# Two one-column fills on GpSimd behind most indirect DMAs, with another table of order

## The chip, the cores and the metric

The kernel runs on one core of a Trainium2 chip. The metric is the time of one execution on the device, in microseconds (us). TensorE does the products, VectorE, ScalarE and GpSimd the work between them, and SyncE (SP) issues the plain loads and stores. GpSimd issues the indirect DMAs, those whose rows go to addresses that a table of indices gives.

## The reference

Two layers follow each other. The first is a gated linear recurrence over time, for each of 4 sequences of 5,056 steps and 256 channels; the second is a mixture of eight experts, over all 20,224 rows of the first one's result. A row whose score with `w_skip` is not above 0 is passed on as it is.

```python
log_a = c * sig_r * np.log(np.clip(a_base, 1e-06, 1.0 - 1e-06))[None, None, :]
a_t = np.exp(log_a)
norm = np.sqrt(np.maximum(1.0 - a_t * a_t, 1e-06))
x_gated = norm * sig_i * x
for t in range(S):
    h = a_t[:, t] * h + x_gated[:, t]
    y[:, t] = h
...
do_compute = x @ w_skip > 0
e_idx = np.argmax(logits, axis=1)          # logits = xc @ w_gate
for e in range(E):                         # E = 8, w1 256x1024, w2 1024x256
    mask = e_idx == e
    h = np.maximum(xc[mask] @ w1[e], 0.0)
    y[mask] = gate_w[mask, None] * (h @ w2[e])
out[do_compute] = xc + y
```

## The kernel before

**Groups and spans.** The rows are cut into groups of 512, and two groups make a span; there are 20 spans of eight tiles of 128 rows (the last has six), 158 tiles in all. For each group SP loads r, i and x (`load`), ScalarE applies tanh, exp and square root, TensorE turns the tiles so that time runs along the free axis (`across`), VectorE scans (`scan`), TensorE turns the result back (`back`), and ScalarE or VectorE copies it from PSUM into a row buffer `yr` (`copy`). GpSimd writes the row ids into that buffer (`ids`, an IOTA), SP stores the rows to `out` (`keep`). TensorE then computes the scores of the span, and VectorE and TensorE work out for each row its expert and its place in a sorted list.

**Sends.** When the places of a span are known, GpSimd sends its tiles, one indirect DMA each (`send`, L609), from `yr` into `xs`, a buffer in DRAM that is sorted by expert. There are three buffers `yr`, and a buffer is free again when its sends have read it.

**Slots.** A slot is one expert's work on 128 or 256 sorted rows: SP fetches them from `xs` (`fetch`, L692) into one of three buffers `xr`, TensorE turns them (`turn`, L706), ScalarE and VectorE make two half-precision parts (`turn_hi`, `turn_lo`), TensorE makes the first product (`mm1`, L727), ScalarE and VectorE the rectified parts (`relu`, L737, and `rest`, L741), TensorE the second product (`mm2`, L753), VectorE weighs it and adds the row (`weighed`, L763), and GpSimd puts 128 rows at a time at their place in `out` with an indirect DMA (`put`, L769). There are 48 slots in a fixed list, `STREAM`, which says for each the span that must have been sent, the expert and the number of rows; eight more follow, one for each expert, and a loop behind them for rows that are left. A buffer `xr` is free when its puts have been read out. 82 puts and 158 sends appear in the profile.

**Weights.** All of the experts' weights are loaded in pieces and turned into two half-precision parts in SBUF: the upper one by ScalarE (L670) or GpSimd (L672), the lower one by VectorE (L676).

**What sets the order.** Each step is a task of a plan, with the engine it runs on, the tasks that must come first and the buffers that it takes. Where a task may run on one of two engines, a letter of the string `ENGINES` says which. The table `ORDER` lists the numbers of all 2,780 tasks, and `Plan.order` goes through it and issues one after the other; each engine then does its instructions in that order:

```python
tasks = [self.tasks[int(i)] for i in ORDER.split()]
...
with tc.manual_schedule():
    for t in plan.order():
        t.f()
```

An instruction that waits holds up all that stands behind it in its engine's queue. Semaphores between engines are set by the framework from what each instruction reads and writes. Between the sends and the fetches they are declared by hand: a fetch waits for the last send of the span that it needs.

Of the kernel before, what the change touches and what calls it, by code (L numbers as in the profile page):

```python
# [22 lines left out]
    "PADDAAAAPAAAADAADAAADAAAAADAPAAAAADAAAAAAAAAAAAADAAAAAADAADADADAADDAADAAADDDAAADDAADAPAAADAAAAAAADPA"  # L23
    "AAADDAPDAADDAAAADAAAADDADAAAAADAAPADADAAPAAAAAAPPAAAPAAAAAAPAPAAAPPPAAAAAAAAPPPPPPAPPPPPPAAAAAAAPPAP"
# [190 lines left out]
def kernel(  # L215
# [12 lines left out]
    nc = tc.nc  # L228
# [372 lines left out]
    def count(s):  # L601
        nt = tiles_in(s)
        nc.vector.tensor_tensor(bases[s + 1], bases[s], vs.pop(s)["rk"][:, nt, :], op=ALU.add)
        known[s] = len(scattered), len(kept)

    def send(s, c):

        g, j = tile_at(s, c)
# [525 lines left out]
```

## Time and profile before

| | |
|---|---|
| time, median of 3 runs | 765.91 us (763.94 to 770.52) |
| time of the profiled execution | 764.61 us |
| span of its profile | 762.8 us |
| mean granted clock of TensorE | 0.948 |

The span runs from the first to the last instruction; the time of the profiled execution has 1.8 us around it. Engines are named PE (TensorE's products), PEld (its weight loads), DVE (VectorE), ACT (ScalarE), POOL (GpSimd) and SP. A row of a timeline ends with the idle time of the engine just before the instruction and with what released it; "issue" stands for time in which it waited for nothing that the profile shows. The granted clock is the share of TensorE's full speed that it was given, 1.00 for 2.4 GHz and 0.50 for 1.2.

### The profile page before, as it was taken

What the parts mean: (1) busy time and instruction counts of PE and PEld (TensorE: products, weight loads), DVE (VectorE), ACT (ScalarE), POOL (GpSimd) and SP (SyncE); (2) the same over time, 40 slices, a digit from 0 to 9 for tenths busy, and PEclk for the clock granted to TensorE, in tenths of its full rate; (3) what the DMA queues carried; (4) which work ended last, traced back from release to release, by engine and by line L of the source; (5) the groups of instructions that cost most, each with busy time, mean ns of one, the idle gap of its engine ahead of it and who ended that gap; (6) DMA issues with size and microseconds to landing.
All of it is one profiled execution on the core that took longest, in us unless ns stands there. A gap on an engine that the chain in (4) does not pass through costs nothing. (4 is left out here: it accounts for less than half of the span.)

```text
span 762.8 us, 16493 instructions
## 1 busy us (share of the span) xinstructions
PE 660.5 (87%) x6304; PEld 561.1 (74%) x6304; DVE 492.5 (65%) x1082; ACT 434.1 (57%) x622; POOL 307.1 (40%) x332
## 2 busy tenths in 40 slices
PE   2565887988989989898998997979987799999996
PEld 2343676877878977777777785769876698989996
DVE  2998885977887757785667576447664365454432
ACT  7889775877887557575664773453725123222231
POOL 5365634445355154375164434412553411321211
PEclk9878598999999999999899998989998899999999
DMA  8899967778876465385546471615353211232110
GB/s 322 311 286 330 301 211 242 236 233 271 273 263 229 158 223 179 111 300 189 196 125 181 165 265 59 198 34 185 133 162 96 83 57 37 97 138 71 56 40 20
DMA packets 72752, 134.73 MB, mean 177 GB/s; under 512 B 9912, under 2 KB 43176, under 8 KB 72672
## 3 DMA queue, kind: packets, MB, share of 16 engines
q1 hardware_dynamic: 60816, 112.84, 45.0%
q0 software_dynamic: 11584, 20.82, 7.7%
q8 instruction: 50, 0.82, 0.5%
q14 instruction: 30, 0.25, 0.1%
q10 hardware_dynamic: 272, 0.00, 0.0%
HBM read 89.75 MB, written 54.71 MB: 189 GB/s over the span
## 5 line engine op out<-in xcount | busy, mean ns | idle before, releaser
L727 PE MATMUL phs<-xhs,wsb 128*128 128x128 f16 (+1 forms) x2688 | 248.3, 248 | 19.6 <-issue 15.6
L753 PE MATMUL pos<-wsb,hps 128*128 128x256 f16 x1968 | 243.8, 276 | 13.7 <-ACT hps L737 5.4
L727 PEld LDWEIGHTS <-wsb 128*128 128x128 f16 x2688 | 210.8, 100 | 43.6 <-issue 28.9
L753 PEld LDWEIGHTS <-hps 128*128 128x128 f16 x1968 | 193.0, 99 | 46.6 <-issue 12.2
L609 POOL DMA_INDIRECT xs<-yr,di x158 | 176.4, 1117 | 110.2 <-issue 45.5
L737 ACT ACTIVATE hps<-phs 128x512 f16<-128x512 f32 x164 | 96.4, 595 | 192.0 <-PE phs L727 106.4
L769 POOL DMA_INDIRECT out_dram<-ots,xrs x82 | 87.0, 1061 | 267.7 <-DVE ots L763 163.8
L741 DVE SCALAR_TENSOR_TENSOR hps<-phs,hps 128x512 f16<-128x512 f32 x164 | 111.3, 685 | 82.1 <-ACT hps L737 77.3
L438 DVE TENSOR_TENSOR_SCAN a<-a,a,m 128x512 f32<-128x512 f32 (+1 forms) x78 | 99.7, 1288 | 0.4
L401 ACT ACTIVATE a<-pt,cc 128x512 f32<-128x512 f32 (+1 forms) x80 | 59.7, 773 | 34.5 <-PE pt L397 15.5
L397 PE MATMUL pt<-ident,i 128*128 128x128 f32 x316 | 53.6, 302 | 22.8 <-DVE i L427 9.8
L716 DVE SCALAR_TENSOR_TENSOR xhs<-pxs,xhs 128x256 f16<-128x256 f32 (+1 forms) x56 | 30.5, 546 | 53.9 <-ACT xhs L713 38.2
L763 DVE SCALAR_TENSOR_TENSOR ots<-pos,xrs 128x256 f32<-128x256 f32 x82 | 38.1, 478 | 40.6 <-PE pos L753 29.3
L397 PE MATMUL pt<-ident,r 128*128 128x128 f32 x316 | 52.2, 304 | 12.6 <-ACT r L388 11.6
L432 DVE SCALAR_TENSOR_TENSOR m<-m,pt 128x512 f32<-128x512 f32 x80 | 53.1, 672 | 14.2 <-PE pt L397 11.5
L397 PEld LDWEIGHTS pt<-ident,i 128*128 128x128 f32 x316 | 40.2, 155 | 29.5 <-issue 10.9
L455 PE MATMUL py<-ident,a 128*128 128x128 f32 x316 | 54.8, 302 | 4.7 <-DVE m L432 2.3
L713 ACT ACTIVATE xhs<-pxs 128x256 f16<-128x256 f32 (+1 forms) x56 | 27.0, 482 | 54.4 <-PE pxs L706 45.2
L427 DVE SCALAR_TENSOR_TENSOR i<-i,x 128x1024 f32<-128x1024 f32 (+1 forms) x40 | 49.6, 1242 | 8.0 <-ACT i L388 7.4
L397 PEld LDWEIGHTS pt<-ident,r 128*128 128x128 f32 x316 | 41.7, 159 | 15.4 <-issue 7.5
L455 PEld LDWEIGHTS py<-ident,a 128*128 128x128 f32 x316 | 45.6, 209 | 8.6 <-DVE m L432 3.0
L676 DVE SCALAR_TENSOR_TENSOR wsb<-w,wsb 128x512 f16<-128x512 f32 x64 | 44.0, 698 | 12.0 <-POOL wsb L672 6.2
(100 smaller groups left out, 577.9 us busy)
## 6 DMA issues: line engine op xcount, KB each, us to landing
r<-in_r_gate_dram SPq DMA_DIRECT2D x39, 512.0 KB
i<-in_i_gate_dram SPq DMA_DIRECT2D x39, 512.0 KB
x<-in_x_dram SPq DMA_DIRECT2D x39, 512.0 KB
out_dram<-yr SPq DMA_DIRECT2D x39, 512.0 KB
w<-in_moe_w_dram SPq DMA_DIRECT2D x64, 256.0 KB
xrs<-xs SPq DMA_DIRECT2D x26, 258.0 KB
xrs<-xs SPq DMA_DIRECT2D x30, 129.0 KB
xs<-yr,di POOLq DMA_INDIRECT x158
```

Of the source, the lines that this page charges most:

```text
L397: nc.tensor.transpose(tile_of(to[g, k], g, j), t[g][:, j, k * P:(k + 1) * P], ident)
L401: nc.scalar.activation(ta[g][:, k, :tiles_of(g) * P], tp.pop((g, k)), AF.Exp, scale=c, bias=c)
L427: nc.vector.scalar_tensor_tensor(ti[g], ti[g], 1.0, tx.pop(g), op0=ALU.add, op1=ALU.mult)
L432: nc.vector.scalar_tensor_tensor(m, m, 0.5e-3, tp.pop((g, k)), op0=ALU.max, op1=ALU.mult)
L438: nc.vector.tensor_tensor_scan(a, a, tm[g][:, k, :n], prev, op0=ALU.mult, op1=ALU.add)
L455: nc.tensor.transpose(pt[:, j, k * P:(k + 1) * P], tile_of(ta[g][:, k, :tiles_of(g) * P], g, 2 * h + j), ident,)
L609: i = nc.gpsimd.indirect_dma_start(out=xs[:, :], out_offset=bass.IndirectOffsetOnAxis(ap=vs[s]["di"][:, c:c + 1], axis=0), in_=yrow[g][:, ...
L727: nc.tensor.matmul(ph[:, c, :], lhsT=self.w.w1(k, part, q * self.fp + c), rhs=self.xx[:, xx, k, :], start=(n == 0), stop=(n == 3 * KD - 1),)
L737: nc.scalar.activation(hh[:, 0], self.h[q][0], AF.Relu)
L741: nc.vector.scalar_tensor_tensor(hh[:, 1], ph, 0.0, hh[:, 0], op0=ALU.max, op1=ALU.subtract)
L753: nc.tensor.matmul(self.po[:self.np, j, :], lhsT=hh[:, h, c, j * P:j * P + self.np], rhs=self.w.w2(f, part), start=(f == 0 and j == 0 and ...
L769: i = nc.gpsimd.indirect_dma_start(out=out[:, :], out_offset=bass.IndirectOffsetOnAxis(ap=self.at[:, j, :], axis=0), in_=self.ot.pop(j)[:s ...
```

## The change

A function `pause` makes two fills of the same one-column buffer `still` on GpSimd. It is called behind each send of span 4 and later and behind each put of slot 3 and later in the list (`PACE`). The loop's slots are not paced. The fills are not tasks of the plan; they are issued inside `send` and `put`. The strings `ENGINES` and `ORDER` are others, of which the diff shows the first line each; the tasks, the buffers and `STREAM` are the same.

```diff
--- before.py
+++ after.py
-    "PADDAAAAPAAAADAADAAADAAAAADAPAAAAADAAAAAAAAAAAAADAAAAAADAADADADAADDAADAAADDDAAADDAADAPAAADAAAAAAADPA"
...
+    "PAAAAADAPDAAADAAAAAADAAAADDAPAAAAAAAAAADDAAAADAADAAAADADAAADAADAADDDDAPAAADDAAAADADDPADADDDAADAAADAA"
...
 ORDER = """
...
+0 6 9 10 12 1620 17 7 1614 1605 1566 18 1621 4 1615 1 2 3 1622 20 11 21 23 15 22 13 1616 8 1623 1626 1567 14 1606 1624
...
+
+PACE = (4, 3)
...
+    still = const.tile([P, 1], F32, name="still")
+
+    def pause():
+
+        for _ in range(2):
+            nc.gpsimd.memset(still, 0.0)
+
     def send(s, c):
...
         scattered.append(i.ins)
+        if s >= PACE[0]:
+            pause()
...
-            self.h, self.ot = {}, {}
+            self.h, self.ot, self.paced = {}, {}, False
...
             tc.add_to_no_dep_group("sent", i.ins)
+            if self.paced:
+                pause()
...
             slot = Slot(f"s{k}", rows)
+            slot.paced = k >= PACE[1]
```

The order of GpSimd's instructions at the sends of span 18, before. `yr36` and `yr37` are the row buffers of its two groups, `di18` its places, `ots35_0` and `ots36_0` results of slots 35 and 36; what an instruction waits for stands at its end.

```order
L443 IOTA yr36_8072 128x4 [waits DMAHW1_49,DMASW7_49,DMASW3_49]
L443 IOTA yr37_8061 128x4
L769 DMA out_0_dram<-ots35_0_8069,xrs35_7669 20224x256 [waits DMAHW4_49,DMASW6_49,DVE_49]
L609 DMA xs_69<-yr36_8072,di18_8059 164096x258 [waits DVE_49,Activation_49,Pool_49]
L609 DMA xs_69<-yr37_8061,di18_8059 164096x258 [waits DVE_49,DMASW0_49,Activation_49,Pool_49]
...
L609 DMA xs_69<-yr36_8072,di18_8059 164096x258 [waits DMASW5_49]
L609 DMA xs_69<-yr37_8061,di18_8059 164096x258 [waits DMASW6_49]
L769 DMA out_0_dram<-ots36_0_8294,xrs36_7931 20224x256 [waits DMAHW5_49,DMASW7_49,DVE_49]
```

The same place after the change:

```order
L779 DMA out_0_dram<-ots35_0_8391,xrs35_7961 20224x256 [waits DMAHW6_49,DMASW6_49,DVE_49]
L612 MEMSET still_123 128x1 [waits Pool_49] x2
L444 IOTA yr37_8384 128x4 [waits DMAHW5_49,DMASW7_49]
L617 DMA xs_69<-yr36_8039,di18_8238 164096x258 [waits DVE_49]
L612 MEMSET still_123 128x1 [waits Pool_49] x2
L617 DMA xs_69<-yr36_8039,di18_8238 164096x258 [waits DMASW0_49]
...
L617 DMA xs_69<-yr36_8039,di18_8238 164096x258 [waits DMASW5_49]
...
L617 DMA xs_69<-yr37_8384,di18_8238 164096x258 [waits DMASW6_49]
L612 MEMSET still_123 128x1 [waits Pool_49] x2
L779 DMA out_0_dram<-ots36_1_8676,xrs36_8113 20224x256 [waits DMAHW0_49,DMASW7_49,DVE_49]
```

The eight sends and the put behind them are the same, in another order of tiles. Two fills stand behind each DMA, the second one waits for GpSimd's own semaphore, and the next DMA follows it. The put of slot 35 with its fills now stands ahead of the id write of `yr37`.

The second place is the end of the sends, also on GpSimd: the six of span 19 with the results of slots 41 to 43. L871 and L872 are two fills of the task `nobody`, which writes a block of empty rows. Before:

```order
L769 DMA out_0_dram<-ots41_1_8970,xrs41_8682 20224x256 [waits DMASW0_49]
L443 IOTA yr38_8517 128x4
L443 IOTA yr39_8785 128x2
L609 DMA xs_69<-yr38_8517,di19_8797 164096x258 [waits DMASW1_49,DVE_49,Pool_49]
...
L609 DMA xs_69<-yr38_8517,di19_8797 164096x258 [waits DMASW4_49]
L871 MEMSET none1_9138 128x516
L872 MEMSET none1_9138 128x2 [waits Pool_49]
L609 DMA xs_69<-yr38_8517,di19_8797 164096x258 [waits DMASW5_49]
L609 DMA xs_69<-yr39_8785,di19_8797 164096x258 [waits DMASW6_49]
L769 DMA out_0_dram<-ots42_1_9179,xrs42_8878 20224x256 [waits DMAHW2_49,DMASW7_49,DVE_49]
L769 DMA out_0_dram<-ots42_0_9174,xrs42_8878 20224x256 [waits DMASW0_49]
```

After the change, where those two are L883 and L884:

```order
L779 DMA out_0_dram<-ots42_0_9481,xrs42_9217 20224x256 [waits DMAHW2_49,DMASW1_49,DVE_49]
L612 MEMSET still_123 128x1 [waits Pool_49] x2
L444 IOTA yr38_9078 128x4
L444 IOTA yr39_9072 128x2
L779 DMA out_0_dram<-ots42_1_9484,xrs42_9217 20224x256 [waits DMASW2_49,DVE_49]
...
L617 DMA xs_69<-yr38_9078,di19_9320 164096x258 [waits DMASW3_49,DVE_49,Activation_49]
...
L617 DMA xs_69<-yr38_9078,di19_9320 164096x258 [waits DMASW7_49]
L612 MEMSET still_123 128x1 [waits Pool_49] x2
L883 MEMSET none1_9636 128x516
L884 MEMSET none1_9636 128x2 [waits Pool_49]
L617 DMA xs_69<-yr38_9078,di19_9320 164096x258 [waits DMASW0_49]
...
L779 DMA out_0_dram<-ots43_0_9683,xrs43_9307 20224x256 [waits DMAHW3_49,DMASW1_49,DVE_49]
```

The two puts of slot 42 stood behind the last six sends and now stand ahead of them, with their fills; the fills of `nobody` stand ahead of the last send instead of in the middle.

## Rows read from the trace of the kernel before

**Rows 1.** Parts 1 and 2 of the page: busy microseconds of each engine, with their share of the span and the count of instructions; and TensorE's busy share, in tenths, in the 40 slices of the span.

```profile
PE 660.5 (87%) x6304; PEld 561.1 (74%) x6304; DVE 492.5 (65%) x1082; ACT 434.1 (57%) x622; POOL 307.1 (40%) x332
PE   2565887988989989898998997979987799999996
```

**Rows 2.** The waits of TensorE's weight loads from 150 to 680 us: line, what was waited for, microseconds in all, times, longest.

```profile
PEld L727 <- issue: 22.3, 30, 2.4
PEld L753 <- issue: 10.9, 15, 1.3
```

**Rows 3.** The timeline of GpSimd from 589 to 600 us, first and last of eight sends: start, length, instruction, and in brackets the idle time before it with what ended it.

```profile
589.92 0.99 POOL L609 DMA_INDIRECT xs<-yr,di  x1 [3.84 <-DVE hps L741]
...
598.95 0.98 POOL L609 DMA_INDIRECT xs<-yr,di  x1 [0.30 <-issue]
```

**Rows 4.** The timeline of TensorE's weight loads over the end of the same run; loads without a gap are one row, with their count.

```profile
598.44 0.28 PEld L727 LDWEIGHTS <-wsb 128*128 128x128 f16 x5 [1.16 <-issue]
599.88 0.26 PEld L727 LDWEIGHTS <-wsb 128*128 128x128 f16 x4 [1.15 <-issue]
601.30 0.88 PEld L727 LDWEIGHTS <-wsb 128*128 128x128 f16 x9 [1.17 <-issue]
```

**Rows 5.** TensorE in eight stretches, the last of them and the sum: stretch, its length, TensorE's busy time and instructions, the share of the clock that was granted, the share of the DMA engines, GB/s.

```profile
...
596.00:605.00 9.00, 4.68 (x36) 0.77 0.13 45
sum 76.00, PE 42.39; mean PE 5.30
```

**Rows 6.** The same in five other stretches that hold a run of sends, the first two and the sum.

```profile
207.40:221.40 14.00, 12.94 (x116) 1.00 0.82 265
231.30:244.40 13.10, 12.50 (x134) 1.00 0.73 230
...
sum 73.80, PE 72.05; mean PE 14.41
```

**Rows 7.** GpSimd's timeline from 536 to 551 us, where ten indirect DMAs and two id writes (IOTA) stand; the rows left out are DMAs of 0.97 to 0.99 us and one IOTA.

```profile
536.79 0.99 POOL L609 DMA_INDIRECT xs<-yr,di  x1 [6.39 <-ACT hps L737]
...
539.26 0.16 POOL L443 IOTA yr<- 128x4 int32 x1
539.59 1.64 POOL L609 DMA_INDIRECT xs<-yr,di  x1 [0.17 <-issue]
...
544.10 1.56 POOL L609 DMA_INDIRECT xs<-yr,di  x1 [0.30 <-issue]
...
549.80 0.97 POOL L609 DMA_INDIRECT xs<-yr,di  x1 [0.30 <-issue]
```

**Rows 8.** GpSimd's timeline at 665 us.

```profile
664.80 0.98 POOL L609 DMA_INDIRECT xs<-yr,di  x1 [0.30 <-issue]
665.77 0.56 POOL L871 MEMSET none<- 128x516 f32 x1
666.38 0.10 POOL L872 MEMSET none<- 128x2 int32 x1
667.13 0.99 POOL L609 DMA_INDIRECT xs<-yr,di  x1 [0.65 <-issue]
```

**Rows 9.** TensorE in five stretches of 8 us each behind a stall, and from 605 us to the end of the products; columns as in rows 5.

```profile
363.00:371.00 8.00, 7.24 (x50) 0.64 0.45 163
466.00:474.00 8.00, 7.29 (x47) 0.67 0.08 19
500.00:508.00 8.00, 6.27 (x41) 0.67 0.13 36
575.00:583.00 8.00, 6.28 (x47) 0.66 0.16 54
602.00:610.00 8.00, 7.11 (x46) 0.64 0.09 33
605.00:757.00 152.00, 151.19 (x1601) 0.99 0.21 66
```

**Rows 10.** GpSimd from 146 to 605 us: the stretch, its length, busy time and instructions; and the two groups of indirect DMAs in it (count, busy time, mean ns of one, idle time before them).

```profile
146.00:605.00 459.00, 199.87 (x209) 0.96 0.55 182
L609 POOL DMA_INDIRECT xs<-yr,di x120 | 130.1, 1085 | 85.4 <-issue 31.4 <-DVE hps L741 17.6 <-ACT hps L737 13.0
L769 POOL DMA_INDIRECT out_dram<-ots,xrs x49 | 53.3, 1088 | 136.7 <-DVE ots L763 69.1 <-DVE yr L465 19.5 <-DVE sg L558 13.9
```

**Rows 11.** The waits of SP's queue, the largest.

```profile
SPq L692 <- DMA out_dram<-ots,xrs: 171.3, 30, 19.5
```

**Rows 12.** GpSimd's timeline: the first put behind each of four runs of sends, with the idle time ahead of it.

```profile
285.78 0.97 POOL L769 DMA_INDIRECT out_dram<-ots,xrs  x1 [3.20 <-DVE ots L763]
371.10 0.99 POOL L769 DMA_INDIRECT out_dram<-ots,xrs  x1 [8.48 <-DVE ots L763]
473.99 0.99 POOL L769 DMA_INDIRECT out_dram<-ots,xrs  x1 [9.31 <-DVE ots L763]
603.96 0.98 POOL L769 DMA_INDIRECT out_dram<-ots,xrs  x1 [4.03 <-DVE ots L763]
```

**Rows 13.** Groups of instructions by line and shape over the whole span: the weight conversion and the copy on ScalarE, and the copy on VectorE.

```profile
L670 ACT ACTIVATE wsb<-w 128x512 f16<-128x512 f32 x40 | 24.7, 627 | 6.9 <-DMA w<-in_moe_w_dram 6.5 <-issue 0.4
L463 ACT COPY yr<-py 128x512 f32<-128x512 f32 x55 | 31.8, 581 | 17.6 <-PE py L455 13.9 <-issue 2.7 <-PE pt L397 0.8
L465 DVE COPY yr<-py 128x512 f32<-128x512 f32 x24 | 16.4, 683 | 8.0 <-PE pt L397 5.4 <-PE py L455 2.4 <-issue 0.2
```

More of the change, by code (lines that the diff above doesn't have):

```diff
@@ L22 @@
 ENGINES = (
-    "PADDAAAAPAAAADAADAAADAAAAADAPAAAAADAAAAAAAAAAAAADAAAAAADAADADADAADDAADAAADDDAAADDAADAPAAADAAAAAAADPA"
-    "AAADDAPDAADDAAAADAAAADDADAAAAADAAPADADAAPAAAAAAPPAAAPAAAAAAPAPAAAPPPAAAAAAAAPPPPPPAPPPPPPAAAAAAAPPAP"
+    "PAAAAADAPDAAADAAAAAADAAAADDAPAAAAAAAAAADDAAAADAADAAAADADAAADAADAADDDDAPAAADDAAAADADDPADADDDAADAAADAA"
+    "AAAADAAADADDAPDDAADAADDAAAPADDDDAAAAAAAPAAAPAAAAAAAAAAAAAAAAAPAAAAAPAAAAPAPAPPPAPPAPPPPPPAAAAPAAPAAA"
     "AAA"
```

220 rows, old and new, of the table ORDER are left out of this document.

## The prediction

> **What bounds the kernel now.** I read the page's busy table and slices first: TensorE is busy 660.5 of 762.8 us, and after the first quarter nearly every slice has it at 80% or more [rows 1]. So time goes where TensorE stands still, and the second view is its waits from 150 to 680 us. The largest are of weight loads that wait for "issue", that is for nothing the profile shows: 22.3 us at the first product and 10.9 us at the second [rows 2]. The timelines of GpSimd and of TensorE's weight loads, side by side, tell where. From 589.92 to 599.9 us GpSimd issues eight sends in a row, one each 1.29 us (0.98 busy, 0.30 idle) [rows 3]. TensorE works through the first five; then it does four or five loads, stands 1.16 us, does four or five more, until 601.3, 1.4 us after the last send [rows 4]. No semaphore holds it.
>
> The same picture stands at the end of eight runs of such DMAs between 270 and 605 us. I cut the stretch from the stall's start to its end out of each: 76.0 us together, TensorE busy 42.4 [rows 5]. Five other stretches with a run of sends in them, 73.8 us together, have it busy 72.05 [rows 6]. What sets those apart is spacing. Between 536.8 and 550.8 us ten DMAs took 14.0 us, 1.40 each, two of them lasting 1.56 and 1.64 us [rows 7]; and the run that begins at 660.9 is cut in the middle by two fills, 1.35 us from one DMA's end to the next one's start [rows 8]. The stalled runs have 1.28 to 1.29 us from DMA to DMA. TensorE's clock adds to it: behind five of the stalls the granted share is 0.64 to 0.67 over 8 us, that is 1.2 instead of 2.4 GHz for about two thirds of the stretch, after TensorE had stood still; from 605 to 757 us, with no long run, it is busy 151.19 of 152.0 at 0.99 [rows 9].
>
> **The change, part by part. The fills.** 126 sends (158 less the 32 of the first four spans) and 79 puts (82 less the three of slots 0 to 2) get two fills each: 205 pairs, 410 fills. A fill of this kind lasts 0.10 us. The order shows that the second waits for the first one's semaphore, as L872 waits for L871 in the trace, which cost 0.05 us there; the DMA behind L872 began 0.65 us after it [rows 8], while the one behind an id write began after 0.17 [rows 7]. A pair then makes 0.10 + 0.05 + 0.10 + 0.17 = 0.42 us from DMA to DMA at the low end and 0.10 + 0.05 + 0.10 + 0.65 = 0.90 at the high end, in place of 0.30: 0.12 to 0.60 us more. I take 0.60, since a fill that waits for a fill and then an indirect DMA is that very row. So the spacing becomes 0.97 + 0.90 = 1.87 us (1.39 at the low end), at or above the 1.40 of the undisturbed run.
>
> *What it returns.* If the stalled stretches become like the others, TensorE's idle time there falls from 33.6 us to 2.4% of 76.0, 1.8 us: a gain of 31.8 us. The clock: in the five stretches of 8 us it is at the lower level for (5 - 3.28) x 8 x 2 = 27.5 us; TensorE is busy in 34.2 of the 40 us, so for 23.5 us of work at half speed, which costs 11.8 us. I count half of it, 6 us, since other gaps stay and one can still let the clock fall.
>
> *What it costs.* GpSimd is idle for 459 - 199.9 = 259 us between 146 and 605 us, and the 169 DMAs there take 169 x 0.60 = 101 us more [rows 10], so it does not become the bound on the whole. But a run of eight takes 4.8 us longer (1.0 at the low end), and what is queued behind it comes later: the puts, and behind them SP's fetches, which wait for a put to land before they get a buffer (171.3 us in 30 waits) [rows 11]. The cover is GpSimd's own idle time before the first put behind a run: 3.20, 8.48, 9.31 and 4.03 us in four runs [rows 12]. Against 4.8 it leaves 1.6, 0, 0 and 0.8, a mean of 0.6 us. Over 16 spans: 9.6 us, which I charge in full, though SP's wait need not be TensorE's; with the low price it is 0, without cover 16 x 4.8 = 77 us.
>
> **The order table.** TensorE's rows are the same products in nearly the same places. Seven evacuations go from ScalarE to VectorE and five weight conversions from GpSimd to ScalarE: ScalarE gains at most 5 x 0.63 = 3.1 us, before the seven it gives away, and VectorE 6 x 0.68 = 4.1 us and one smaller copy [rows 13]; VectorE, the busier of the two, is busy 65% of the span [rows 1], so nothing. At the end the last six sends now stand behind the puts of slot 42 instead of ahead of them, and with the fills take about 12 us until the slots that need them can be fetched; I count nothing for it, 3 us as the bound. For every other place that the table moves I have no row; I keep 8 us (1%) to either side, and 0 as the value.
>
> **Sum.** The profiled execution took 764.6 us (span 762.8 and 1.8 around it): 764.6 - 31.8 - 6 + 9.6 = 736.4. The median of the runs shown is 1.3 us above it: **738 us**.
>
> **Rivals.** *The stall has another cause.* Runs of sends stand where a span's work ends, so they may only coincide with it. For it: the runs at 207 and 231 us, at 1.0 share of the clock and a DMA share of 0.73 to 0.82, stall little [rows 6], so spacing and DMA load are not told apart. Against: TensorE's stalled pieces come at the same pace whichever line it works on, and begin after the same five or six DMAs. Then nothing comes back, and the lateness stays between 0 and 9.6 us: 766 to 775.
>
> The Trainium skill, "SBUF — State Buffer", section "Who interferes with whom", states that only the port pair that VectorE and GpSimd share causes contention, that a DMA never contends with a compute engine and that TensorE and ScalarE wait for nobody. By that rule GpSimd's DMAs cannot hold TensorE, spacing them returns nothing, and this rival holds. The rows on TensorE during runs [rows 3 to 6] speak against it, though they show a coincidence and no cause.
>
> *Slower: the spacing makes the fetches late.* The place is GpSimd's queue at the end of each span, the mechanism the 4.8 us by which the puts behind eight sends slip, with SP's fetch and TensorE's next slot behind them. From 43.6/16 = 2.7 us per span on it eats all that is gained (31.8 + 11.8). For it: SP waits for puts longer than for anything else [rows 11]. Against: the idle time ahead of those puts [rows 12]. At three quarters of 4.8, 3.6 us per span, it gives 764.6 + 57.6 - 43.6 = 778.6, about 780.
>
> *Half of it.* The fills hide in the 0.30 us that the DMAs wait anyway, or the pace of 1.39 is still too close, and stalls shrink to half: 764.6 - 16 - 3 + 2 = 747.6, so 749. The change would then not do what it says, or not fully.
>
> **How the numbers follow.** A measurement of this kernel tells about 1%, 7.7 us, from no change (its three runs span 764 to 770). Forecast 0.64; half of it 0.12; another cause 0.14; late fetches 0.10. The forecast's own range is 738 less 6 (the other half of the clock), 9.6 (no lateness) and 8 (the table), hence 716 at the lowest since not all come at once, and 750 upward. The whole reaches 770 at the top, which takes in half the cases of another cause. Faster by over 1%: 0.64 + 0.12 = 0.76; within 1%: 0.11 of another cause; slower: 0.10 + 0.03 = 0.13.
>
> **What would show it.** Right: 410 fills on GpSimd, DMAs of a run at 1.4 to 1.9 us; in the runs after 270 us weight loads no longer stand about 1.2 us for "issue", their total from 150 to 680 us falls from 33 to under 15 us at the two product lines; the clock falls at most twice after 350 us. Wrong: the same pieces of four or five loads at the wider spacing (another cause), a spacing still at 1.3 us (hidden fills), or longer waits of SP for puts with TensorE waiting for a fetched slot (late fetches).

## The result, and the profile after

The changed kernel took 690.93 us (687.92 to 694.14, four runs) beside 765.17 for the kernel before (763.94 to 770.52): 0.902 of the time, 95% interval 0.896 to 0.908. The forecast was 738 us with a range of 716 to 770: the direction holds, the size doesn't, and the time lies below the range.

The unchanged kernel before took 757 to 773 us in five of the thirteen comparisons made for this study, the first one among them (called the upper level below), and 688 to 689 in the other eight (the lower level); one chip showed both, so each experiment is given with the time of the kernel before beside it.

The profiled execution after took 691.65 us, its span 689.8, at a mean granted clock of 0.974. Busy times and TensorE's slices from the page, which answer to [rows 1]:

```profile
PE 635.7 (92%) x6304; PEld 551.8 (80%) x6304; DVE 494.1 (72%) x1089; ACT 431.8 (63%) x620; POOL 346.9 (50%) x737
PE   2756698998999999999999999999999999999996
```

From the eleventh slice on TensorE is busy 90% or more in every slice but the last. Of the 73.0 us that the span lost, TensorE's busy time gave 660.5 - 635.7 = 24.8 with the same 6,304 products, and its idle time 102.3 - 54.1 = 48.2. From 146 to 605 us, first before and then after (stretch, length, busy time and instructions, granted clock, DMA share, GB/s):

```profile
146.00:605.00 459.00, 410.83 (x3889) 0.96 0.55 182
```

```profile
146.00:605.00 459.00, 451.79 (x4461) 1.00 0.56 186
```

In the same 459 us it is idle for 7.2 us instead of 48.2, the clock is at 1.00, and 572 more instructions are done. The waits of weight loads for issue from 150 to 680 us, after, which answer to [rows 2]:

```profile
PEld L737 <- issue: 4.7, 8, 0.9
PEld L763 <- issue: 4.4, 6, 1.1
```

That is 9.1 us in place of 33.2. GpSimd's timeline in a run of DMAs, after:

```profile
496.44 0.97 POOL L617 DMA_INDIRECT xs<-yr,di  x1 [0.66 <-issue]
497.40 0.28 POOL L612 MEMSET still<- 128x1 f32 x2
498.34 0.97 POOL L617 DMA_INDIRECT xs<-yr,di  x1 [0.65 <-issue]
...
500.32 0.97 POOL L779 DMA_INDIRECT out_dram<-ots,xrs  x1 [0.74 <-issue]
```

A pair of fills lasts 0.28 us and the next DMA begins 0.65 us behind it, so DMAs of the run follow each other by 1.90 us. Two puts stand in the middle of this run of sends (500.32 and 502.27); in the old table two puts stand inside the same run, two sends later.

### The profile page after: what moved, and what is told of

It is laid out like the page before. It is cut to its first block, busy times and chain, and to the rows that moved or that the text cites. A ratio compares the mean times of both kernels' runs of the same rounds, so it can differ in the third digit from the quotient of the medians.

```text
span 689.8 us, 16890 instructions
## 1 busy us (share of the span) xinstructions
PE 635.7 (92%) x6304; PEld 551.8 (80%) x6304; DVE 494.1 (72%) x1089; ACT 431.8 (63%) x620; POOL 346.9 (50%) x737
## 4 chain that ended last, share of the span: by engine, by line
PE 70%; DMA 8%; DVE 8%; issue 6%; ACT 5%; POOL 2%; SPq 0%; DVEq 0%; ACTq 0%; POOLq 0%
PE phs L737 26%; PE pos L763 26%; PE pt L398 6%; PE lg L495 5%; PE py L456 4%; DMA w<-in_moe_w_dram 3%; PE pxs L716 2%; DMA out_dram<-ots,xrs 2%; DVE wsb L686 1%; DVE a L439 1%; DMA xrs<-xs 1%; DMA i<-in_i_gate_dram 1%; DVE hps L751 1%; ACT a L402 1%; DVE i L428 1%
## 5 line engine op out<-in xcount | busy, mean ns | idle before, releaser
L763 PE MATMUL pos<-wsb,hps 128*128 128x256 f16 x1968 | 236.8, 273 | 4.5 <-issue 1.7
L737 PE MATMUL phs<-xhs,wsb 128*128 128x128 f16 (+1 forms) x2688 | 238.6, 244 | 0.9 <-issue 0.4
L737 PEld LDWEIGHTS <-wsb 128*128 128x128 f16 x2688 | 207.1, 98 | 20.8 <-issue 6.4
L763 PEld LDWEIGHTS <-hps 128*128 128x128 f16 x1968 | 190.8, 98 | 32.8 <-issue 6.8
L398 PE MATMUL pt<-ident,r 128*128 128x128 f32 x316 | 49.2, 295 | 16.9 <-ACT r L389 13.4
L398 PE MATMUL pt<-ident,i 128*128 128x128 f32 x316 | 50.2, 298 | 14.0 <-DVE i L428 8.7
L433 DVE SCALAR_TENSOR_TENSOR m<-m,pt 128x512 f32<-128x512 f32 (+1 forms) x80 | 53.0, 670 | 4.2 <-PE pt L398 3.8
L398 PEld LDWEIGHTS pt<-ident,r 128*128 128x128 f32 x316 | 39.4, 152 | 20.1 <-issue 9.5
L612 POOL MEMSET still<- 128x1 f32 x410 | 45.7, 111 | 11.8
```

Source lines behind the costliest of these rows:

```text
L398: nc.tensor.transpose(tile_of(to[g, k], g, j), t[g][:, j, k * P:(k + 1) * P], ident)
L433: nc.vector.scalar_tensor_tensor(m, m, 0.5e-3, tp.pop((g, k)), op0=ALU.max, op1=ALU.mult)
L737: nc.tensor.matmul(ph[:, c, :], lhsT=self.w.w1(k, part, q * self.fp + c), rhs=self.xx[:, xx, k, :], start=(n == 0), stop=(n == 3 * KD - 1),)
L763: nc.tensor.matmul(self.po[:self.np, j, :], lhsT=hh[:, h, c, j * P:j * P + self.np], rhs=self.w.w2(f, part), start=(f == 0 and j == 0 and ...
```

## The experiments

**Table and fills apart.** I call stops what [rows 4] and [rows 5] show: TensorE's weight loads wait for "issue" again and again at the end of a run of close DMAs. The first theory was the prediction's: DMAs that stand close stop TensorE, and the fills set them apart. Its rival: the new table is the gain, and the fills came with it. The first run is the changed kernel without fills:

```diff
-PACE = (4, 3)
+PACE = (99, 99)
```

> The changed kernel without a single fill: the new table of order alone. Spacing theory (indirect DMAs that follow each other by 1.28 us take TensorE's work away, the fills set them apart): the stalls come back, TensorE's weight loads wait for issue over 25 us at the two product lines, granted clock near 0.95, 745 to 775 us. Order theory (the table put the sends and fetches where they do no harm, the fills only come with it): 690 to 705 us and few waits for issue.

The second is the kernel before with `pause`, its two calls and `PACE = (4, 3)`, and its own table:

```diff
+        for _ in range(2):
+            nc.gpsimd.memset(still, 0.0)
...
+        if s >= PACE[0]:
+            pause()
...
+            if self.paced:
+                pause()
```

> The kernel before, its own table, with the two fills behind the same DMAs. Spacing theory: 690 to 710 us, granted clock 0.97, waits for issue at the two product lines under 20 us. Order theory: 755 to 785 us, since the old table was made without fills and the puts come later. In between, by the forecast's own sum (stalls back, half the clock, 9.6 us of lateness): 738.

Measured: the table alone 686.41 us, the fills alone 748.47, and the kernel before, beside them, 688.85 (lower level): ratios 0.996 (0.993 to 0.999) and 1.089 (1.083 to 1.094). Neither theory had this: there was nothing to gain here, the table returned 0.4%, and the fills cost 60 us. So both kernels were run again.

> The kernel before, unchanged, on the chip of the other runs. If its stops of TensorE without a wait (14.7 us between 146 and 605 us) and its long waits for products that were long done (31.3 us) belong to the program, they come again: 755 to 775 us, granted clock about 0.95. If they belong to the chip or the day it was measured on, they are gone: 685 to 700 us, and the table and the fills must be weighed anew against that.

> The changed kernel, unchanged, on the same chip: 686 to 694 us, as when it was first timed, whichever theory holds.

Measured, in one comparison: 689.25 us and 687.98, both the same as the kernel before (1.000, 0.997 to 1.003, and 1.000, 0.998 to 1.002). The stops are not in this trace of the kernel before. The run of sends of [rows 3] stands there again, with two puts behind it. First the first send and the two puts on GpSimd's timeline, then TensorE in that stretch:

```profile
524.01 0.98 POOL L609 DMA_INDIRECT xs<-yr,di  x1 [2.48 <-DVE hps L741]
...
534.33 0.98 POOL L769 DMA_INDIRECT out_dram<-ots,xrs  x1 [0.30 <-issue]
535.62 0.98 POOL L769 DMA_INDIRECT out_dram<-ots,xrs  x1 [0.31 <-issue]
```

```profile
524.00:538.00 14.00, 14.00 (x154) 1.00 0.43 141
```

Ten DMAs stand 1.29 us apart, and TensorE is busy for 14.00 of 14.00 us. In [rows 5] it had 4.68 of the 9.00 us at the end of the same run. Close DMAs alone do not stop it. The upper level came again in later comparisons. The new table without fills:

> The new table without fills once more, to meet a chip on which the kernel before takes 765 to 775 us instead of 689. There the spacing theory expects stops of TensorE without a wait at the ends of the runs of sends and 740 to 770 us; if the new table avoids them by itself, 685 to 695 us. Where the kernel before takes 689: 684 to 689, as before.

Measured: 759.24 us beside 773.32, ratio 0.980 (0.966 to 0.993). The stops are there. The last of eight sends of that same run on GpSimd, and TensorE's weight loads around it:

```profile
585.11 0.97 POOL L617 DMA_INDIRECT xs<-yr,di  x1 [0.31 <-issue]
```

```profile
584.73 0.42 PEld L763 LDWEIGHTS <-hps 128*128 128x128 f16 x4 [0.61 <-issue]
586.17 0.19 PEld L763 LDWEIGHTS <-hps 128*128 128x128 f16 x2 [1.02 <-issue]
```

From 150 to 680 us the loads of the two products wait 47.2 us for issue, against 33.2 in [rows 2]. The longest of these waits has another reason. TensorE's load, then its transposes of a fetched slot and the copy of them that ScalarE makes for the next product:

```profile
488.12 0.10 PEld L737 LDWEIGHTS <-wsb 128*128 128x128 f16 x1 [8.27 <-issue]
```

```profile
476.95 0.61 PE L716 MATMUL pxs<-ident,xrs 128*128 128x128 f32 x4
487.47 0.60 ACT L723 ACTIVATE xhs<-pxs 128x512 f16<-128x512 f32 x1 [12.40 <-remote]
```

The row names issue, but the product that stands there needs `xhs`, and ScalarE wrote it from 487.47 to 488.07 us. ScalarE had been idle for 12.40 us, and the transposes had ended at 477.56. TensorE stood 8.27 us because ScalarE was late, from the fifth DMA of a run at about 1.3 us until 1.6 us after its last.

The old table with the fills:

> The old table with two fills once more. Where the kernel before takes 765 to 775 us, the spacing theory expects no stop of TensorE without a wait, and the price of late fetches that the old table paid elsewhere: about 748 us, with the same waits as in the first run of this kernel. If the fills cure nothing there, the stops and the late fetches add up: 800 us or more. Where the kernel before takes 689: 748 again.

Measured: 754.73 us beside 764.44, ratio 0.993 (0.986 to 1.001). The stops are gone: from 150 to 680 us the weight loads of the two products wait 10.7 us for issue, with the new table alone 47.2. The first two rows are of the old table with fills, the next two of the new table alone:

```profile
PEld L764 <- issue: 8.1, 7, 3.2
PEld L738 <- issue: 2.6, 3, 0.9
```

```profile
PEld L737 <- issue: 29.7, 27, 8.3
PEld L763 <- issue: 17.5, 29, 1.8
```

The four combinations, in us, each with the kernel before beside it in brackets:

| | upper level | lower level |
|---|---|---|
| old table, no fills | 765.17 | 689.25 (689.18) |
| new table, no fills | 759.24 (773.32) | 686.41 (688.85) |
| old table, two fills | 754.73 (764.44) | 748.47 (688.85) |
| new table, two fills | 690.93 (765.17) | 687.98 (689.18) |

Read by rows, the level costs 76 and 73 us without fills, and 6 and 3 with them: the fills remove what the upper level costs. Read by columns, the fills cost the old table 60 us at the lower level and the new one 2. At the upper level each half of the change returns little without the other (0.7 and 2.0%).

**Where the old table pays.** The old table was run with fills behind its sends alone, `PACE = (4, 99)`, and behind its puts alone, `PACE = (99, 3)`.

> The old table with fills behind its sends alone (126 pairs). The old table with all fills took 748 us beside 689 without. If that price is paid where a run of eight sends takes 4.8 us longer and the puts and fetches behind it come late (the rival of late fetches), nearly all of it is here: 735 to 750 us. If it is the sum of small delays behind every DMA, 126 of 205 pairs: about 725. If the kernel before takes 765 on this chip, as it did when it was first profiled, and stalls follow from close sends, this kernel is faster than it there.

> The old table with fills behind its puts alone (79 pairs). Late fetches behind long runs of sends: little of the price is here, 689 to 697 us, since puts stand in ones and twos. Small delays behind every DMA: 79 of 205 pairs of 59 us, about 712 us.

Measured: sends alone 734.37 us beside 688.1 (1.068, 1.063 to 1.073), puts alone 689.98 beside 689.33 (1.001, 0.999 to 1.003), both at the lower level. So the price is paid in the runs of sends, 46 us; the fills behind puts add 14 only beside the others. The place of it, in the old table with all fills at the lower level: GpSimd, then the chain of work behind it (start, length, what).

```profile
478.85 0.98 POOL L618 DMA_INDIRECT xs<-yr,di  x1 [0.72 <-ACT xhs L724]
...
493.01 0.98 POOL L618 DMA_INDIRECT xs<-yr,di  x1 [0.65 <-issue]
495.07 1.52 POOL L780 DMA_INDIRECT out_dram<-ots,xrs  x1 [0.80 <-DVE mx L542]
```

```profile
495.07 2.97 DMA out_dram<-ots,xrs
...
498.23 2.92 DMA xrs<-xs
```

```profile
501.29 1.09 PE L717 MATMUL pxs<-ident,xrs 128*128 128x128 f32 x4 [4.89 <-DMA xrs<-xs]
```

Eight sends take from 478.85 to 493.99 us; the put queued behind them begins at 495.07 and lands at 498.04; SP's fetch, which waits for the put, is issued at 498.23; and TensorE stands 4.89 us until the fetched rows are there. In the changed kernel two puts stand inside this run, behind its second send. Over the span the transposes of fetched slots wait for their rows like this, first in the kernel before at the lower level, then in the old table with fills behind sends alone, then with all fills, then in the changed kernel:

```profile
PE pxs L706 <- DMA xrs<-xs: 1.6, 2, 0.9
```

```profile
PE pxs L717 <- DMA xrs<-xs: 12.6, 9, 2.8
```

```profile
PE pxs L717 <- DMA xrs<-xs: 22.8, 11, 4.9
```

```profile
PE pxs L716 <- DMA xrs<-xs: 4.4, 6, 1.7
```

So 21 of the 60 us are seen directly as waits for late rows. How the rest follows from them, in TensorE's other waits and in a lower clock (0.956 for 0.975), the runs do not separate.

**One fill.** `range(1)` in place of `range(2)`, in the old table and in the new one:

> The old table with one fill in place of two behind the same 205 DMAs. In the trace of the changed kernel a pair lasts 0.21 us and the next DMA begins 0.65 after it; without the wait of the second fill the gap may be 0.17 to 0.65, so 1.25 to 1.75 us from DMA to DMA. Late fetches: the price of 59 us goes with the added time, from 5 us at 1.30 to 50 at 1.75.

> The changed kernel with one fill in place of two. In the old table one fill hid in the 0.30 us that the next DMA waited anyway, so the pace stays at about 1.28 us. On a chip on which the kernel before takes 689 us: 685 to 690, as without fills. On a chip on which it takes 765 to 775: the spacing theory expects stops of TensorE without a wait at the ends of the runs of sends and 740 to 770 us; if the new table avoids the stops by itself, 685 to 695.

Measured: old table 781.04 us beside 771.92 (upper level; 1.011, 1.003 to 1.020), new table 686.57 beside 688.72 (lower level; 0.998, 0.996 to 1.000). The first run shows why one fill does nothing at the upper level:

```profile
606.73 0.98 POOL L618 DMA_INDIRECT xs<-yr,di  x1 [0.19 <-issue]
607.70 0.13 POOL L613 MEMSET still<- 128x1 f32 x1
608.02 0.98 POOL L618 DMA_INDIRECT xs<-yr,di  x1 [0.19 <-issue]
```

```profile
608.73 0.33 PEld L764 LDWEIGHTS <-hps 128*128 128x128 f16 x4 [1.20 <-issue]
610.19 0.17 PEld L738 LDWEIGHTS <-wsb 128*128 128x128 f16 x3 [1.13 <-issue]
```

The fill lies in the 0.30 us that the next DMA waited anyway; the pace stays at 1.29 us, and TensorE does three or four loads and stands 1.13 to 1.20 us, as in [rows 4]. A fill that changes no spacing changes no stop: the stops go with the distance, not with the fill. The ten DMAs of [rows 7], without a fill at 1.40 us each, fit this: TensorE is busy for 16.00 of the 16.00 us around them, from 536.8 us on. No run makes the distance by other means than fills.

**Sends or puts, with the new table.** The changed kernel with fills behind one kind of DMA, `PACE = (4, 99)` and `PACE = (99, 3)`:

> The changed kernel with fills behind its sends alone (126 pairs), none behind puts. Spacing theory: the runs are of sends, so nearly all of the gain stays, 690 to 702 us. If any pair of DMAs that stands close does harm, puts too, about 79 of 205 pairs of the gain are gone: 715 to 725 us.

> The changed kernel with fills behind its puts alone (79 pairs), none behind sends. Spacing theory: runs of sends stand 1.28 us apart again and TensorE stalls at their ends: 740 to 770 us, like the new table without fills. Order theory: as the changed kernel, 690 to 700 us.

Both came at the lower level, where nothing is to be gained: 688.17 and 687.97 us beside 688.85 (0.999 and 1.000). They were run again with the changed kernel:

> The changed kernel itself once more, together with the two that follow. Where the kernel before takes 765 to 775 us: 688 to 694, no stop of TensorE without a wait behind 146 us, if spacing and the new table together are what the gain needs. Where it takes 689: 688.

> The new table with fills behind its puts alone. Where the kernel before takes 765 to 775 us: the runs are of sends, so stops come as without fills, 745 to 765 us. Where it takes 689: 688.

> The new table with fills behind its sends alone. Where the kernel before takes 765 to 775 us: the stops are gone, 688 to 696 us, if runs of sends alone cause them; 705 to 725 if each close pair of DMAs costs its share. Where it takes 689: 688.

Again the lower level: 688.33, 687.51 and 687.42 us beside 689.25. A third time, one by one:

> The new table with fills behind its sends alone, once more. Where the kernel before takes 765 to 775 us: 688 to 696 us and no stop of TensorE without a wait, if runs of sends alone cause them; 705 to 725 if each close pair of DMAs costs its share. Where it takes 689: 688.

Measured, at the upper level: 690.30 us beside 757.50, ratio 0.915 (0.911 to 0.919). From 150 to 680 us its two products wait little for issue:

```profile
PEld L737 <- issue: 5.3, 8, 0.9
PEld L763 <- issue: 4.3, 7, 0.9
```

The fills behind the sends do all that the change does there.

> The new table with fills behind its puts alone, once more. Where the kernel before takes 755 to 775 us: the runs of sends stand at 1.28 us, so the stops stay and it takes 745 to 765 us, like the table without fills (759). Where it takes 689: 688.

This one met the lower level: 684.76 us beside 687.60 (0.995, 0.992 to 0.998). What the fills behind puts do by themselves at the upper level was not seen.

**How much the new table covers.** Six fills in place of two, `range(6)`:

> The changed kernel with six fills in place of two: four more, each after the one before, at 0.10 us and about 0.05 to 0.1 between them, so 0.6 to 0.8 us more from DMA to DMA and about 2.6 us spacing. If the new table hides the fills because its fetches stand far enough ahead of their use (late fetches), its reserve is used up here as the old table's was by two: 720 to 760 us. If it hides them because GpSimd's time does not matter to it, 688 to 695.

Measured: 780.83 us beside 688.75 (lower level; 1.133, 1.128 to 1.138). GpSimd's timeline, then the waits of transposes for a fetched slot:

```profile
502.11 0.98 POOL L617 DMA_INDIRECT xs<-yr,di  x1 [0.66 <-issue]
503.08 0.91 POOL L612 MEMSET still<- 128x1 f32 x6
504.64 1.00 POOL L617 DMA_INDIRECT xs<-yr,di  x1 [0.65 <-issue]
```

```profile
PE pxs L716 <- DMA xrs<-xs: 31.5, 13, 6.5
```

At 2.53 us from DMA to DMA the new table waits 31.5 us for late fetches, as the old one waited 22.8 at 1.90. Its cover ends between the two.

## Why the prediction was wrong in size

**The spacing**: right. I took 0.60 us more and 1.87 from DMA to DMA; it is 1.90. The high bound, from the fill that waits for a fill [rows 8], was the right row.

**Fills remove the stops**: right, with a condition I could not see in one trace. The stops come at the upper level only; there the fills remove them with either table, at 1.90 us, and one fill at 1.29 us does not. My rival of another cause is half true: at the lower level the same runs stop nothing, so something beside the spacing must be present, and no run shows what it is.

**What the stops cost**: this term failed first. I summed the idle time of eight stretches and half of a clock loss read in five, 31.8 + 6 = 37.8 us. The two levels of the kernel before differ by 765.17 - 689.25 = 75.9. Its span at the lower level is 688.3, TensorE's busy time 631.1:

```profile
PE 631.1 (92%) x6304; PEld 550.3 (80%) x6304; DVE 493.3 (72%) x1082; ACT 433.6 (63%) x622; POOL 311.8 (45%) x332
```

Beside [rows 1] that is 45.1 us less of idle time, where I had 31.8, and 29.4 less of busy time for the same products, where I read 11.8 and counted 6. The idle time outside the chosen stretches, 13 us, came with the upper level as well. Of the busy time the clock accounts for about 19 us: weighed with the granted clock in stretches of 1 us, 28 us are lost to it at the upper level and 10 at the lower. I had looked only behind five stalls, at stretches I had chosen. A part of the rest is made by the stops themselves. In the run of [rows 4]:

```profile
593.60 1.50 PE L727 MATMUL phs<-xhs,wsb 128*128 128x128 f16 x24
...
599.87 0.38 PE L727 MATMUL phs<-xhs,wsb 128*128 128x128 f16 x4 [1.03 <-issue]
```

Four products by themselves count 0.38 us, of 24 in a row four count 0.25.

**The lateness**: I charged 9.6 us, after a cover read from four places [rows 12]. The new table pays 2, the old one 60, 46 of it behind sends. That is my rival of late fetches, mechanism and place, though not in the kernel that I forecast; that I had priced it at 57.6, with three quarters of 4.8 us, was luck, since no row gave the three quarters. The cover I read was largely made by the upper level. Three of the four puts at the lower level (the fourth, at 534.33 above, has 0.30 us):

```profile
264.14 1.05 POOL L769 DMA_INDIRECT out_dram<-ots,xrs  x1 [0.30 <-issue]
338.51 0.99 POOL L769 DMA_INDIRECT out_dram<-ots,xrs  x1 [0.88 <-DVE ots L763]
428.70 0.99 POOL L769 DMA_INDIRECT out_dram<-ots,xrs  x1 [2.56 <-DVE ots L763]
```

Against 4.8 us these leave 4.5, 3.9, 2.2 and 4.5, a mean of 3.8, and over 16 spans an estimate of 61 us; the fills behind sends alone cost 46, all of them 60. A wait that a stall makes longer is no cover for what removes the stall.

**The order table**: 0 with 8 us to either side, and this is the other term that failed. Where the fills are, it is worth 748.47 - 687.98 = 60.5 us at the lower level and 754.73 - 690.93 = 63.8 at the upper one, by comparisons that differ in the kernel before by up to 1 us. I read it by TensorE's rows, which hardly move. What the table saves is seen in the waits for fetched rows, 4.4 us for 22.8 with the fills. The place is probably GpSimd's queue, where 13 puts for nine now stand inside a span's sends from span 4 on; no run moved them alone, so this is argued and not shown. For the seven evacuations and five conversions I had nothing, and the table without fills returns 0.4% at the lower level, which leaves little for them.

**The sum**: mine was 38 us of gain, 9.6 of lateness and no table. The runs have 76 of gain and 2 of lateness with the new table. The 47 us between 738 and 691 are 38 of stops undervalued and 8 of lateness overcharged, within about a us. The mechanism and the direction were right; the step that failed is the size of the stops, 37.8 us in my sum and 75.9 measured.

At the lower level TensorE is busy 14.00 of 14.00 us under ten close DMAs; at the upper level two fills behind GpSimd's DMAs took the new table from 759.24 to 690.93 us. The rule of the Trainium skill ("SBUF — State Buffer", "Who interferes with whom") that TensorE and ScalarE wait for nobody and that no DMA contends with an engine is stated there for SBUF's ports. It fits the lower level; at the upper one it does not foretell the time, and the traces do not tell by which path TensorE and ScalarE are held.

The signs I had named came as written: 410 fills, 1.90 us from DMA to DMA in a run, 9.1 us of waits for issue where I asked for under 15, and the clock at 1.00 between 146 and 605 us. They tell that the stops are gone, not what they had cost.

## What to carry to other kernels

Where an engine stands without a wait while GpSimd issues a run of indirect DMAs, time the same program on several occasions before explaining it, then spread the run: two dependent one-column fills made 1.90 us of 1.29, while one fill vanished in the gap. Spreading delays whatever is queued behind the run on GpSimd, so price that with the stops gone, and order the queue anew for it; here, at the upper level, one half without the other returned 0.7 and 2.0%, both together 10. With the new table, fills behind the sends were enough. At the lower level the change returned nothing.

## What the runs showed of the hardware

The same program ran at 689 us or at 757 to 773, on a single core, and chip 11 did both. At the upper level TensorE stops inside a product, mostly for 0.4 to 1.4 us at a time with a few loads between, from the fifth to the seventh indirect DMA of a run at 1.29 us on until 1 to 2 us after its last. Other engines are late as well, and this costs more. In the kernel before, TensorE is idle for 48.2 us from 146 to 605 us; its products wait 17 us of it for issue and about 30 for ScalarE and VectorE, while at the lower level the idle time of this stretch is 6 us in all. The two largest waits at the upper level:

```profile
PE phs L727 <- issue: 10.5, 23, 1.0
PE pos L753 <- ACT hps L737: 5.4, 1, 5.4
```

The second is one wait. A product ended at 491.48 us, and ScalarE, idle from 491.8 us on, began on it at 500.96, when the run of DMAs (485.2 to 499.2 us) had ended, and TensorE's next product waited for ScalarE:

```profile
490.12 1.36 PE L727 MATMUL phs<-xhs,wsb 128*128 128x256 f16 x11 [0.38 <-issue]
...
501.61 1.76 PE L753 MATMUL pos<-wsb,hps 128*128 128x256 f16 x6 [5.37 <-ACT hps L737]
```

```profile
500.96 0.60 ACT L737 ACTIVATE hps<-phs 128x512 f16<-128x512 f32 x1 [9.19 <-remote]
```

So it is not TensorE alone that is held. What is held, whether instructions on their way to an engine or the news that a product is done, the traces do not tell, nor why a chip is in one level or the other; this stays open.
